# Eleven hidden-layer steps of the last chunk in seven products, with three banks, in a fused scan and feed-forward kernel

## The chip, the core and the metric

The kernel runs on one core of one Trainium2 chip. The metric is the device time in microseconds of one execution; three runs of the kernel before are given, and their median is the time to compare with. Engines are named as the profile names them: PE (TensorE, with PEld for its weight loads), DVE (VectorE), ACT (ScalarE), POOL (GpSimd) and SP (SyncE, which only issues transfers).

## What is computed

The program is a state-space scan (the "attention" block) whose output goes through a feed-forward block with a cosine gate. The feed-forward block is what the change touches:

```
# scan output y: (4, 8, 768, 32), brought to x: 3072 tokens x 256
h = x @ w_in             # 3072 x 256  times  256 x 2048
g = h * np.cos(h)
out = g @ w_out          # 3072 x 2048 times 2048 x 256
```

All numbers are float32. A float32 matrix product is two passes of a matmul on PE here: the profile shows twice as many MATMUL rows as the program has products.

## The kernel before

The 3072 tokens are cut into NC = 6 chunks (128 time steps of four sequences, 512 tokens each). A chunk's scan output lies transposed in `yT`, as two units `u` of 256 tokens with two 128-row halves `k` of the model dimension. For each chunk there are NF = 16 steps; a step `n` belongs to chunk `c = n // 16` and treats one unit `u` and one pair of 128-wide columns of `w_in`, numbered `j` (0 to 7). So the last chunk has steps 80 to 95, the last half-unit steps 88 to 95.

A step is a chain over all engines:

- `first(n)` (L650): `hp`, a PSUM bank of 128 partitions by 512, is filled by four products of 128 x 128 with 128 x 256 (two column blocks `e`, two rows `k`).
- `wind_k` (L664, ACT) and `wind_w` (L669, DVE) bring h to turns; `gate` (L679, ACT) takes the sine; `gated` (L683, DVE) makes `gT` = h times the cosine, and is the last to read the `hp` bank.
- `differ` (L707, POOL) makes four differences `gd` of the quarters of `gT` in three operations.
- `second(n)`, from chunk 1 on `seven(n)` (L741), multiplies by `w_out`. The 2 x 2 blocks of this product are done in seven block products for eight (the Winograd form of Strassen's scheme): seven products of 128 x 128 with 128 x 128, on sums and differences of blocks, accumulated in seven PSUM places over the eight steps of a half-unit. At the end of a half-unit ACT copies the places to `ps`, and `rest` (L779) makes four DVE sums of them and stores the result. The `w_out` sums (`wd`) are made once, by POOL.

The order on each engine is the order in which the Python code issues instructions; nothing is rescheduled, and waits between engines are put in by the framework from what tiles are written and read. In the main loop (L999 to L1094) step `n` issues `first(n)`, `wind(n)`, `gate(n)`, `gated(n)`, work of the scan for later chunks, and then `second(n - LAG)` with LAG = 2. So PE's row is: hp of step n, the seven products of step n - 2, hp of step n + 1, and so on.

[...] two pairs under the tag "scan" (used by the scan, and by `pair`), two banks "h" for `hp`, two banks "o" for the second layer's places. A bank taken under a tag is the one used two takings ago, so `hp` of step n waits for `gated` of step n - 2. The last half-unit takes its places `lo` and `hi` from two pairs and `mid` from a bank "o".

At the end, `shared` (L795) sums `mid` after step 94's products, and `last_step` (L807) adds the last step's product straight to the result: PE, one DVE add, two transfers, for each of two halves.

Of the kernel before, what the change touches and what calls it, by code (L numbers as in the profile page):

```python
# [25 lines left out]
def kernel(  # L26
# [17 lines left out]
    P = 128  # L44
# [630 lines left out]
    def wind(n):  # L675
        wind_k(n)
        wind_w(n)

    def gate(n):  # L679
        cos = turns[n]  # L680
        ACT.activation(cos, cos, AF.Sin, bias=quarter, scale=TWO_PI)  # L681
# [25 lines left out]
    def differ(n):  # L707
# [5 lines left out]
        G.tensor_tensor(out=d[:, 2], in0=g[:, 0], in1=d[:, 0], op=ALU.subtract)  # L713
        G.tensor_tensor(out=d[:, 3], in0=g[:, 2], in1=d[:, 2], op=ALU.subtract)  # L714

    unit_rows = out.rearrange("(s q k i) m -> q k i s m", s=2, q=2, i=W)

    def second(n):
# [20 lines left out]
    def seven(n):  # L739

        c = n // NF  # L741
        u, j = turn_of(n)
        final = n >= NC * NF - NJ
        if j == 0:


            if final:
                lo, hi = (pair("o")[:, 0].rearrange("p (q m) -> p q m", m=P) for _ in range(2))
                mid = bank([P, 4, P], "o", "o")
                o[c, u] = (mid, lo, hi, {1: mid[:, 0], 6: mid[:, 1], 7: mid[:, 2], 5: mid[:, 3],  # L750
                                         2: lo[:, 0], 3: lo[:, 1], 4: hi[:, 0]})
# [12 lines left out]
        a_ = {1: g[:, 0], 2: g[:, 2], 3: d[:, 3], 4: g[:, 3], 5: d[:, 0], 6: d[:, 2], 7: d[:, 1]}  # L764
        starts = (1, 2, 4) if final else (1, 7)
        for q in (1, 2, 6, 7, 5, 4, 3):
            PE.matmul(at[q], lhsT=a_[q], rhs=w[q], start=(j == 0 and q in starts),  # L767
                      stop=(j == NJ - 1), skip_group_check=True)
# [7 lines left out]
        ACT.copy(out=ps[:, 0:3], in_=o[c, u][0][:, 0:3])  # L776
        ACT.copy(out=ps[:, 3:7], in_=o[c, u][1])

        def rest():  # L779
            for dst, a_, b_ in ((sum_[:, 0:2], ps[:, 1:3], ps[:, 0:1]),  # L780
                                (sum_[:, 5:7], ps[:, 3:5], sum_[:, 0:1]),
                                (sum_[:, 3:5], ps[:, 5:3:-1], sum_[:, 5:6]),
                                (sum_[:, 2:3], ps[:, 6:7], sum_[:, 6:7])):
                V.tensor_tensor(out=dst, in0=a_, in1=b_.to_broadcast([P, dst.shape[1], P]),  # L784
                                op=ALU.add)
            for s in range(2):
# [155 lines left out]

    AHEAD = 4

    def first_steps():
# [53 lines left out]
    for n in range(AHEAD, NC * NF + LAG):  # L999
        c, f = divmod(n, NF)  # L1000
        if n < NC * NF:

            if c > 0 and f in (loads_of := (6, 7, 8, 9) if c == 1 else (0, 1, 2, 3)):
                load(c + 2, loads_of.index(f))
            if n in (NF - 4, NF - 3):
                load_arow(n - NF + 8)
            if n == NF - 2:
                for k in (4, 5):
                    for s in range(2):
                        load_x(k, s)  # L1010
            if n in (NF - 1, NF):
                load_along(2, (2 * (n == NF), 2 * (n == NF) + 1))
            for e, i in chunks_at(n, "along"):
                load_along(e + 1, (2 * i, 2 * i + 1))
            first(n)
            closing = f == NF - 1 and 1 <= c < NC - 1
            take_y = finish2(c + 1) if closing else None
            wind(n)
            if closing:
                take_y(0)  # L1020
            for e, s in chunks_at(n - 1, "turn"):
                turn2(e, s)
            for k in units_at(n, 2):
                turn_unit(k)
            if n + 1 in piece:
                rests_of.append(grade(*piece[n + 1], later=True))
            gate(n)
            while len(rests_of) > (n == AHEAD):
                rest = rests_of.pop(0)
                if rest:  # L1030
                    rest()
            joins = n in piece and piece[n] in held
            if joins:
                join(*piece[n])

            behind = [lambda at=at: decays2(*at) for at in decays_at(n)]
            behind += [lambda k=2 * c - 1 + i: add_state(k) for c, i in chunks_at(n, "state")]
            behind += [lambda c=c, b=2 * s + p: reaches(c, b) for c, s in chunks_at(n, "reach")
                       for p in range(2)]
            behind += [lambda at=at: turn_blocks(*at) for at in chunks_at(n, "turn")]  # L1040
            behind += [lambda k=k, p=p: decays0(k, p) for k, at in unit_at.items()
                       for p in range(2) if at[0][p] == n]
            behind = [lambda k=2 * c + i, q=q: weights(k, q) for c, i in chunks_at(n, "weigh")
                      for q in range(2)] + behind
            behind = [lambda k=k: weights(k, 1) for k in units_at(n - 1, 3)] + behind
            if not joins and behind:
                behind.pop(0)()
            gated(n)
            if closing:
                take_y(1)  # L1050
            if n == NF + 7:
                weigh0(5)
            if add_s and (n == NF - 5 or units_at(n - 1, 4)):
                exchange = add_s()
                add_s = None
            if n == NF + 9:
                exchange()
            for do in behind:
                do()
            if f not in ((10, 11, 12) if c == 1 else (10, 11)):  # L1060
                for do in unsummed:
                    do()
                unsummed.clear()
            for k, ((_, last_), *_) in unit_at.items():
                if last_ == n:
                    weigh0(k)
        for i, js in differ_at.get(n, ()):
            differ_w(i, js)
        if n == AHEAD + 1:
            second(AHEAD - LAG)  # L1070
        if n >= LAG and n != AHEAD:
# [53 lines left out]
```

## Time and profile before

| what | value |
|---|---|
| runs of the kernel before, us | 368.54, 367.84, 368.74 (median 368.54) |
| profiled execution, us | 367.37 |
| its span, from the first to the last instruction, us | 365.2 |
| granted TensorE clock | 0.999 |
| hp products (L659), busy us, count | 182.7, 768 |
| DVE `w` (L672), mean ns | 688 |
| DVE `gT` (L686), mean ns | 683 |
| ACT `k` (L666) and sine (L681), mean ns | 596 and 723 |
| POOL `gd` (L711, L713, L714), mean ns | 757, 483, 557 |

The times are of one execution with the profiler on. Lines of a timeline give the start and the time in us, the engine, the line of the kernel, the operation, what is written from what, the shape and how often; in brackets stands the idle time of the engine before it and what ended it. Lines that stand together on an engine are merged ("x8"), and then the time is that of all of them. A matmul's end is modelled and overlaps the start of the next, so the distance of starts is what counts on PE.

### The profile page before, as it was taken

The numbers are of one execution on the slowest core, as the hardware profiler recorded it, in microseconds if no ns is written. First come the engines' busy times: TensorE is split into PE (matmuls) and PEld (weight loads), VectorE is DVE, ScalarE is ACT, GpSimd is POOL, SyncE is SP. The second block draws the span as 40 slices with busy tenths as digits, with TensorE's granted clock in tenths as the row PEclk, the third lists the DMA queues.
The fourth block names the chain that finished last, engine by engine and source line by source line (L and its number), as shares of the span: only waits on it lengthen the run. The fifth ranks groups of instructions, "written<-read, shape, count | busy, mean of one in ns | idle before, by whom it ended". The sixth has DMA issues, their size and how long they took to land.

```text
span 365.2 us, 9749 instructions
## 1 busy us (share of the span) xinstructions
PE 359.7 (98%) x3902; PEld 324.8 (89%) x3902; DVE 249.6 (68%) x420; ACT 177.8 (49%) x324; POOL 204.5 (56%) x331
## 2 busy tenths in 40 slices
PE   8999999999999999999999999999999999999995
PEld 5788888888999999999989999989999999999995
DVE  7799998488868747967735977754876363644463
ACT  4588766454454355534345444335553534443442
POOL 6567666679766544447734456744355443554441
PEclk9999999999999999999999999999999999999999
DMA  8997865692664455316034210010000010010011
GB/s 146 294 334 154 203 139 72 105 129 64 133 98 65 92 106 72 69 39 121 9 56 62 47 50 22 2 44 5 22 11 0 2 31 2 2 29 3 0 29 31
DMA packets 97324, 26.39 MB, mean 72 GB/s; under 512 B 87328, under 2 KB 93184, under 8 KB 97280
## 3 DMA queue, kind: packets, MB, share of 16 engines
q1 hardware_dynamic: 96032, 25.38, 34.6%
q8 instruction: 31, 0.51, 0.6%
q10 hardware_dynamic: 1248, 0.39, 0.5%
q14 instruction: 13, 0.11, 0.1%
HBM read 22.36 MB, written 3.34 MB: 70 GB/s over the span
## 4 chain that ended last, share of the span: by engine, by line
PE 89%; DVE 4%; POOL 3%; ACT 2%; issue 2%; ACTq 0%; POOLq 0%; DVEq 0%
PE hp L659 42%; PE o L767 33%; PE o L729 5%; PE y L629 2%; PE g L603 1%; PE y L477 1%; DVE mag L261 1%; PE y L617 1%; DVE mag L263 1%; POOL gd L711 1%; PE g L456 1%; PE a_ps L364 1%; PE warm L84 1%; DVE w L672 1%; POOL gd L713 1%
## 5 line engine op out<-in xcount | busy, mean ns | idle before, releaser
L659 PE MATMUL hp<-yT,w_in 128*128 128x256 f32 x768 | 182.7, 381 | 0.3 <-DVE gT L686 0.3
L659 PEld LDWEIGHTS hp<-yT,w_in 128*128 128x128 f32 x768 | 139.5, 190 | 18.2 <-issue 1.0
L711 POOL TENSOR_TENSOR gd<-gT 128x256 f32<-128x256 f32 x79 | 59.8, 757 | 111.9 <-DVE gT L686 102.5
L672 DVE SCALAR_TENSOR_TENSOR w<-hp,k 128x512 f32<-128x512 f32 x96 | 66.1, 688 | 71.4 <-ACT k L666 71.3
L681 ACT ACTIVATE w<-w,quarter 128x512 f32<-128x512 f32 x96 | 69.4, 723 | 71.8 <-DVE w L672 71.5
L666 ACT ACTIVATE k<-hp 128x512 int32<-128x512 f32 x96 | 57.2, 596 | 94.3 <-PE hp L659 94.1
L686 DVE TENSOR_TENSOR gT<-hp,w 128x512 f32<-128x512 f32 x96 | 65.6, 683 | 35.1 <-ACT w L681 33.2
L767 PE MATMUL o<-words,gd 128*128 128x128 f32 x474 | 65.9, 275 | 0.1
L767 PEld LDWEIGHTS o<-words,gd 128*128 128x128 f32 x474 | 59.3, 192 | 0.3 <-POOL gd L713 0.3
L767 PEld LDWEIGHTS o<-w_out,gT 128*128 128x128 f32 x316 | 47.2, 191 | 4.1
L767 PE MATMUL o<-w_out,gT 128*128 128x128 f32 x316 | 48.4, 276 | 0.0
L714 POOL TENSOR_TENSOR gd<-gT,gd 128x128 f32<-128x128 f32 x79 | 44.0, 557 | 6.2
L713 POOL TENSOR_TENSOR gd<-gT,gd 128x128 f32<-128x128 f32 x79 | 38.1, 483 | 6.2
L767 PE MATMUL o<-words,gT 128*128 128x128 f32 x158 | 30.6, 275 | 0.0
L767 PE MATMUL o<-w_out,gd 128*128 128x128 f32 x158 | 30.6, 275 | 0.0
L729 PE MATMUL o<-w_out,gT 128*128 128x256 f32 x128 | 29.9, 379 | 0.0
L375 DVE TENSOR_TENSOR_SCAN lam<-arow,unit 128x512 f32<-128x512 f32 x20 | 28.0, 1400 | 0.0
L729 PEld LDWEIGHTS o<-w_out,gT 128*128 128x128 f32 x128 | 24.2, 190 | 3.3
L767 PEld LDWEIGHTS o<-words,gT 128*128 128x128 f32 x158 | 24.0, 192 | 0.0
L767 PEld LDWEIGHTS o<-w_out,gd 128*128 128x128 f32 x158 | 24.0, 192 | 0.0
L465 DVE TENSOR_TENSOR m<-g,lam 128x512 f32<-128x512 f32 x24 | 16.2, 681 | 0.7 <-PE g L456 0.5
L784 DVE TENSOR_TENSOR sum<-ps,sum 128x256 f32<-128x256 f32 (+1 forms) x27 | 15.1, 586 | 0.6
(109 smaller groups left out, 274.7 us busy)
## 6 DMA issues: line engine op xcount, KB each, us to landing
words<-in_moe_w_in_dram SPq DMA_DIRECT2D x8, 512.0 KB
words<-in_moe_w_out_dram SPq DMA_DIRECT2D x8, 512.0 KB
xr<-in_x_dram SPq DMA_DIRECT2D x24, 128.0 KB
arow<-a_cut SPq DMA_DIRECT2D x10, 256.0 KB
arow<-a_cut SPq DMA_DIRECT2D x10, 252.0 KB
out_dram<-sum SPq DMA_DIRECT2D x18, 128.0 KB
bc<-in_B_dram SPq DMA_DIRECT2D x24, 64.0 KB
blocks<-in_B_dram SPq DMA_DIRECT2D x16, 32.0 KB
```

The costliest lines, as they stand in the source:

```text
L375: V.tensor_tensor_scan(out=lams[k][:, p, hs].rearrange(flat), data0=rows_.rearrange(flat), data1=unit0[:, hs].rearrange(flat), initial=0.0 ...
L465: V.tensor_tensor(out=m, in0=gs[k, q][:, :, 0:2 * P].rearrange("p k (s i) -> p k s i", s=2), in1=l, op=ALU.mult)
L659: PE.matmul(to_[:, e], lhsT=w_in[:, k, fs], rhs=y[:, k], start=(k == 0), stop=(k == KT - 1), skip_group_check=True)
L666: ACT.activation(k, hp[n], AF.Copy, bias=0.25, scale=INV_2PI)
L672: V.scalar_tensor_tensor(out=w, in0=hp[n], scalar=INV_2PI, in1=k, op0=ALU.mult, op1=ALU.subtract)
L681: ACT.activation(cos, cos, AF.Sin, bias=quarter, scale=TWO_PI)
L686: V.tensor_tensor(out=gT[n], in0=hp.pop(n), in1=cos, op=ALU.mult)
L711: G.tensor_tensor(out=d[:, 0:2], in0=g[:, 1:2].to_broadcast([P, 2, P]), in1=g[:, 3::-3], op=ALU.subtract)
L713: G.tensor_tensor(out=d[:, 2], in0=g[:, 0], in1=d[:, 0], op=ALU.subtract)
L714: G.tensor_tensor(out=d[:, 3], in0=g[:, 2], in1=d[:, 2], op=ALU.subtract)
L729: PE.matmul(o[c, u][:, t], lhsT=g[:, 2 * e + t], rhs=w_out[:, 2 * j + e], start=(j == e == t == 0), stop=(j == NJ - 1 and e == 1), skip_gr ...
L767: PE.matmul(at[q], lhsT=a_[q], rhs=w[q], start=(j == 0 and q in starts), stop=(j == NJ - 1), skip_group_check=True)
```

## The change

In steps 83 to 93 (`sevens`, eleven of the sixteen steps of the last chunk) the first layer too is done in seven products of 128 x 128 with 128 x 128. With it come:

- `differ_in`: the sums of `w_in` blocks (`wid`), by POOL in chunk 3, sixteen operations of 128 x 256; `differ_y`: the sums of `yT` blocks of the last chunk (`yd`), four DVE operations after steps 79 and 80.
- `first7`: seven products, then an ACT copy of one of them and four DVE sums that put the four blocks of h together in the `hp` bank. Products 6, 7, 5 and 4 go to a pair of banks `m` that all eleven steps share.
- In these steps `wind_w`, `gate` and `gated` of step n are issued in step n + 1; `wind_w(n - 1)` stands between the first and the second of step n's sums, `gated(n - 1)` after the fourth.
- A third `hp` bank, from a "scan" pair, for every third of the eleven steps (85, 88), from a bank "o" for step 91. The last half-unit takes `mid` and `hi` from one pair, `lo` from a bank "o".
- The second layer's products come in another order: 1, 2, 7, 5, 6, 4, 3 in `sevens`, and 1, 2, 4, 6, 7, 5, 3 in the last half-unit.
- The sums of the half-unit that ends with step 79 stand before and after `wind_w(82)`; those of the one that ends with step 87 go to POOL, one in each of the steps 90 to 93.

```diff
+    def differ_in(i, js):
...
+        g = [win4[:, k, js, e] for k in range(2) for e in range(2)]
+        a_ = (g[1], g[1], g[0], g[2])[i]
+        b_ = (g[3], g[0], wid[0][:, js], wid[min(i, 2)][:, js])[i]
+        G.tensor_tensor(out=wid[i][:, js], in0=a_, in1=b_, op=ALU.subtract)
...
+    def differ_y(c, i):
...
+        V.tensor_tensor(out=d[:, i], in0=a_, in1=b_,
+                        op=ALU.add if i in (1, 2) else ALU.subtract)
...
+    def first7(n, to_, at6, at):
...
+        w = {1: win4[:, 0, j, 0], 2: win4[:, 1, j, 0], 3: wid[3][:, j], 4: win4[:, 1, j, 1],
+             5: wid[0][:, j], 6: wid[2][:, j], 7: wid[1][:, j]}
...
+        dst = {6: at6, 1: to_[:, 0], 7: at[:, 0], 5: at[:, 1], 4: at[:, 2], 3: to_[:, 1],
+               2: to_[:, 0]}
...
+        parts = ms[3].rearrange("p (t q m) -> p t q m", t=2, q=4)[:, n % 2]
+        add = dict(op=ALU.add)
+        for q in (6, 1):
+            product(q)
+        ACT.copy(out=parts[:, 0], in_=to_[:, 0])
+        for q in (7, 5, 4, 3, 2):
+            product(q)
+        V.tensor_tensor(out=parts[:, 1], in0=at6, in1=parts[:, 0], **add)
+
+        def rest():
+            V.tensor_tensor(out=parts[:, 2:4], in0=at[:, 0:2],
+                            in1=parts[:, 1:2].to_broadcast([P, 2, P]), **add)
+            V.tensor_tensor(out=to_[:, 2:4], in0=at[:, 2:0:-1],
+                            in1=parts[:, 2:3].to_broadcast([P, 2, P]), **add)
+            V.tensor_tensor(out=to_[:, 1], in0=to_[:, 1], in1=parts[:, 3], **add)
+
+        return rest
...
-                lo, hi = (pair("o")[:, 0].rearrange("p (q m) -> p q m", m=P) for _ in range(2))
-                mid = bank([P, 4, P], "o", "o")
+                t = pair("o").rearrange("p b (q m) -> p b q m", m=P)
+                mid, hi = t[:, 0], t[:, 1]
+                lo = bank([P, 4, P], "o", "o")
...
-        for q in (1, 2, 6, 7, 5, 4, 3):
+        for q in ((1, 2, 4, 6, 7, 5, 3) if final else (1, 2, 7, 5, 6, 4, 3) if n in sevens else
+                  (1, 2, 6, 7, 5, 4, 3)):
...
+    sevens = range(NC * NF - 13, NC * NF - 2)
+    late, at_ = [], {}
+
+    def first_of_seven(n):
+
+        i = n - sevens[0]
+        if i == 0:
+            at_["hp"] = pair("hp")[:, 0]
+            at_["m"] = pair("m").rearrange("p b (q m) -> p b q m", m=P)
+        if n == NC * NF - NJ + LAG + 1:
+            at_["hp"] = bank([P, TB], "hp", "o")
+        rest = first7(n, at_["hp"] if i % 3 == 2 else bank([P, TB], "hp", "h"),
+                      at_["m"][:, 1, 0], at_["m"][:, 0])
+        if i:
+            wind_w(late[0])
+        rest()
...
-            first(n)
+            if n in sevens:
+                first_of_seven(n)
+            else:
+                first(n)
+                if n - 1 in sevens:
+                    wind_w(n - 1)
+            if n - 1 in sevens:
+                gate(n - 1)
+            finish_late()
...
-            wind(n)
+            wind_k(n)
+            if n == sevens[0] - 1:
+                unsummed[0](range(0, 2))
+            if n not in sevens:
+                wind_w(n)
+            if n == sevens[0] - 1:
+                unsummed.pop()(range(2, 4))
...
-            gate(n)
+            if n not in sevens:
+                gate(n)
...
-            gated(n)
+            if n + 1 in sevens or n in sevens:
+                late.append(n)
+            else:
+                gated(n)
...
+            for i in {sevens[0] - 4: (0, 2), sevens[0] - 3: (1, 3)}.get(n, ()):
+                differ_y(NC - 1, i)
+            if n in sevens and unsummed:
+                i = n - sevens[-1] + 3
+                unsummed[0](range(i, i + 1), G)
+                if i == 3:
+                    unsummed.pop()
...
+        if n // NF == NC - 3:
+            i, q = divmod(f, 4)
+            differ_in(i, slice(2 * q, 2 * q + 2))
```

More of the change, by code (lines that the diff above doesn't have):

```diff
@@ L714, in differ @@
         G.tensor_tensor(out=d[:, 3], in0=g[:, 2], in1=d[:, 2], op=ALU.subtract)
+    win4 = w_in.rearrange("p k (j e f) -> p k j e f", j=NJ, e=2)
+    wid, yd = [], {}
+    def differ_in(i, js):
+        if i == len(wid):
+            t = conv.tile([P, 2 * WC, 2], U32, tag="words", bufs=8, name="wid")
+            wid.append(t.rearrange("p a w -> p (a w)").bitcast(FP32)
+                       .rearrange("p (j f) -> p j f", j=NJ))
+        g = [win4[:, k, js, e] for k in range(2) for e in range(2)]
+        a_ = (g[1], g[1], g[0], g[2])[i]
+        b_ = (g[3], g[0], wid[0][:, js], wid[min(i, 2)][:, js])[i]
+        G.tensor_tensor(out=wid[i][:, js], in0=a_, in1=b_, op=ALU.subtract)
@@ new lines, in differ_y, with product @@
+    def differ_y(c, i):
+        if i == 0:
+            yd[c] = ms[2].rearrange("p (i u m) -> p i u m", i=4, u=2)
+        d = yd[c]
+        y11, y12, y21, y22 = (yT[c][:, :, k, h * P:(h + 1) * P] for k in range(2) for h in range(2))
+        a_ = (y12, y22, y22, y21)[i]
+        b_ = (y11, y12, d[:, 0], d[:, 2])[i]
+        V.tensor_tensor(out=d[:, i], in0=a_, in1=b_,
+                        op=ALU.add if i in (1, 2) else ALU.subtract)
+    def first7(n, to_, at6, at):
+        c, f = divmod(n, NF)
+        u, j = turn_of(n)
+        hp[n] = to_
+        to_ = to_.rearrange("p (q m) -> p q m", q=4)
+        w = {1: win4[:, 0, j, 0], 2: win4[:, 1, j, 0], 3: wid[3][:, j], 4: win4[:, 1, j, 1],
+             5: wid[0][:, j], 6: wid[2][:, j], 7: wid[1][:, j]}
+        d, y = yd[c][:, :, u], yT[c][:, u].rearrange("p k (h i) -> p k h i", h=2)
+        y_ = {1: y[:, 0, 0], 2: y[:, 1, 0], 3: y[:, 1, 1], 4: d[:, 3], 5: d[:, 0], 6: d[:, 2],
+              7: d[:, 1]}
+        dst = {6: at6, 1: to_[:, 0], 7: at[:, 0], 5: at[:, 1], 4: at[:, 2], 3: to_[:, 1],
+               2: to_[:, 0]}
+        def product(q):
+            PE.matmul(dst[q], lhsT=w[q], rhs=y_[q], start=(q in (6, 1, 7)), stop=True,
+                      skip_group_check=True)
+        parts = ms[3].rearrange("p (t q m) -> p t q m", t=2, q=4)[:, n % 2]
[13 more added lines that the diff above has]
+        return rest
@@ L777, in seven, with rest @@
         ACT.copy(out=ps[:, 3:7], in_=o[c, u][1])
[L779 to L786, printed above, removed]
+        def rest(of=range(4), eng=V):
+            for dst, a_, b_ in [((sum_[:, 0:2], ps[:, 1:3], ps[:, 0:1]),
+                                 (sum_[:, 5:7], ps[:, 3:5], sum_[:, 0:1]),
+                                 (sum_[:, 3:5], ps[:, 5:3:-1], sum_[:, 5:6]),
+                                 (sum_[:, 2:3], ps[:, 6:7], sum_[:, 6:7]))[i] for i in of]:
+                eng.tensor_tensor(out=dst, in0=a_, in1=b_.to_broadcast([P, dst.shape[1], P]),
+                                  op=ALU.add)
+            for s in range(2 if 3 in of else 0):
                 nc.sync.dma_start(out=unit_rows[s, 2 * c + u], in_=sum_[s * W:(s + 1) * W, 1:5].rearrange(
@@ L943, with finish_late @@
     AHEAD = 4
+    sevens = range(NC * NF - 13, NC * NF - 2)
+    late, at_ = [], {}
+    def first_of_seven(n):
+        i = n - sevens[0]
+        if i == 0:
+            at_["hp"] = pair("hp")[:, 0]
[7 more added lines that the diff above has]
+        rest()
+    def finish_late():
+        while late:
+            n = late.pop()
+            gated(n)
     def first_steps():
@@ L1047 @@
                 behind.pop(0)()
-            gated(n)
+            if n + 1 in sevens or n in sevens:
+                late.append(n)
+            else:
+                gated(n)
             if closing:
@@ L1059 @@
                 do()
-            if f not in ((10, 11, 12) if c == 1 else (10, 11)):
+            for i in {sevens[0] - 4: (0, 2), sevens[0] - 3: (1, 3)}.get(n, ()):
[5 more added lines that the diff above has]
+                    unsummed.pop()
+            if n not in sevens and f not in ((10, 11, 12) if c == 1 else (10, 11)):
                 for do in unsummed:
```

## The prediction

> **What bounds the kernel now.** I read the busy shares first, then the chain that ended last, then the timeline of TensorE and of the others over the last chunk, where the change acts.
>
> ```profile
> PE 359.7 (98%) x3902; PEld 324.8 (89%) x3902; DVE 249.6 (68%) x420; ACT 177.8 (49%) x324; POOL 204.5 (56%) x331
> PE 89%; DVE 4%; POOL 3%; ACT 2%; issue 2%; ACTq 0%; POOLq 0%; DVEq 0%
> ...
> 315.07 1.89 PE L659 MATMUL hp<-yT,w_in 128*128 128x256 f32 x8
> 316.80 0.61 PE L767 MATMUL o<-w_out,gT 128*128 128x128 f32 x4
> ...
> 318.36 1.89 PE L659 MATMUL hp<-yT,w_in 128*128 128x256 f32 x8
> ...
> 326.93 0.60 ACT L666 ACTIVATE k<-hp 128x512 int32<-128x512 f32 x1 [1.21 <-PE hp L659]
> 327.56 0.69 DVE L672 SCALAR_TENSOR_TENSOR w<-hp,k 128x512 f32<-128x512 f32 x1 [1.05 <-ACT k L666]
> 328.28 0.72 ACT L681 ACTIVATE w<-w,quarter 128x512 f32<-128x512 f32 x1 [0.76 <-DVE w L672]
> 329.11 0.69 DVE L686 TENSOR_TENSOR gT<-hp,w 128x512 f32<-128x512 f32 x1 [0.86 <-ACT w L681]
> 329.94 0.72 POOL L711 TENSOR_TENSOR gd<-gT 128x256 f32<-128x256 f32 x1 [1.50 <-DVE gT L686]
> ```
>
> TensorE never rests: a step lasts 3.29 us (315.07 to 318.36), 1.73 for hp (16 half-width passes' worth in 8) and 1.56 for the fourteen 128-column passes of the seven products, 0.111 a pass. The second thing to see is the slack: gT follows its hp by 4.2 us, but the products that read it start a step later still, so VectorE and ScalarE wait for TensorE, never the reverse. The third is what small DVE and ACT work costs, and what a late wait costs TensorE:
>
> ```profile
> 32.86 0.68 DVE L686 TENSOR_TENSOR gT<-hp,w 128x512 f32<-128x512 f32 x1
> 33.66 1.59 PEld L659 LDWEIGHTS hp<-yT,w_in 128*128 128x128 f32 x8 [0.71 <-POOL mag L249]
> 33.69 1.97 PE L659 MATMUL hp<-yT,w_in 128*128 128x256 f32 x8 [0.33 <-DVE gT L686]
> ...
> 272.27 0.69 DVE L672 SCALAR_TENSOR_TENSOR w<-hp,k 128x512 f32<-128x512 f32 x1 [1.81 <-ACT k L666]
> 272.88 0.68 DVE L465 TENSOR_TENSOR m<-g,lam 128x512 f32<-128x512 f32 x1
> ...
> 338.15 0.72 ACT L681 ACTIVATE w<-w,quarter 128x512 f32<-128x512 f32 x1 [0.76 <-DVE w L672]
> 338.78 0.46 ACT L776 COPY ps<-o 128x384 f32<-128x384 f32 x1
> 339.14 0.59 ACT L777 COPY ps<-o 128x512 f32<-128x512 f32 x1
> ...
> 360.10 0.42 DVE L801 TENSOR_TENSOR ps<-ps 128x256 f32<-128x256 f32 x1
> 360.56 0.29 DVE L803 TENSOR_TENSOR ps<-ps 128x128 f32<-128x128 f32 x1
> 360.77 0.42 DVE L814 TENSOR_TENSOR ob<-o,ps 128x256 f32<-128x256 f32 x1
> ```
>
> A 512-column DVE operation lets the next independent one start after 0.61, a 128-column one after 0.21; a dependent one follows a 256-column add after 0.46. L814, with one operand in PSUM, takes 0.42 like L801 without. ACT's copies follow each other at 0.36 and 0.50 (their time less 0.09). When hp waited for gT, the weight load came 0.12 after gT's end (at the last step 0.05), and its matmul ran 0.1 longer, the load being bare. I take 0.08 plus 0.11.
>
> **What the Trainium skill says.** "TensorE: Matmul & The Clock Gate", "Step-by-step: what each phase is for": weight loads are pulled ahead of running matmuls, matmuls stay in program order, so one waiting product holds all behind it. The trace agrees: loads start 0.11 before their matmuls, and after the wait at 33.66 load and matmul start together. "GPSIMD Engine Reference", Specifications: GpSimd contends with DVE instructions that have two SBUF inputs. Agrees: the L784 sums took 0.41 before and about 0.70 during POOL work, while w, with one PSUM input, stayed at 0.69 beside L711. "PSUM — Partial Sum Buffer", Terms: two engines must not touch a bank at once. No run here shows a collision, but the built program's waits respect whole banks, and that decides below.
>
> **The change, part by part.** Count from T, the first pass of a seven-product hp step; products come as 6, 1, 7, 5, 4, 3, 2, two passes each.
>
> Removed: 14 passes for 16 halves, 1.73 - 1.56 = 0.17 a step, eleven steps: 1.9 us, all on the path.
>
> Added per step: one ACT copy (128 columns: by the rows of 384, 0.460, and 256, 0.379, between 0.20 and 0.30; I take 0.26) and four DVE adds of 128, 256, 256, 128 columns, each with a PSUM input. DVE has room: 0.21+0.61+0.46+0.46+0.21+0.61 = 2.56 of 3.11. Order is the trouble. On DVE a step runs: first sum, w of the step before, second, third, fourth sum, gT of the step before. In the built program the first sum waits not for product 6, which it reads, but for product 4, the last to write that pair of banks; and the next step's product 6, first in its row, waits for the third sum. So:
> - product 4's second pass issues at 9 x 0.111 = 1.00; a result was usable 0.31 (the copy of mid, at 359.15, after a pass issued at 358.84) to 0.38 (k after hp, less its longer pass) after issue: first sum at 1.34;
> - w at 1.55, second sum at 2.16, third at 2.62, its end 3.04;
> - load at 3.12, next matmul at 3.23.
>
> A step is thus 3.23, not 3.11 (bounds 3.17 and 3.30 from the spreads above). The fourth sum starts at 3.08, ends 3.37; gT starts 3.29, ends 3.98; k runs 3.40 to 4.00. In that rhythm the other waits are met: the copy at 0.68 to 0.94 comes just before product 3's load at 1.00; gT's POOL work (0.73, 0.46, 0.46, begun 0.15 after gT) ends 2.7 into the next step, product 3 of the second layer loads at 2.9.
>
> Four hand-overs don't fit the rhythm.
> - Step 83 to 84: hp 84 takes the bank of hp 82, whose gT now stands behind step 83's sums. T is 315.07; the third sum waits for product 2 (316.86), runs at 317.20, fourth 317.66, gT 317.87 to 318.56. Product 1 of step 84 goes at 318.75 for 318.40: this step is 3.46. The output sums now around w of 82 push that w from 314.40 by at most 0.35; product 3 of step 83 would absorb that in the same wait.
> - Step 90: two ps copies of the finished half-unit stand in ACT's row between k of 89 (0.15 on) and the copy of 90. They begin at 0.66 and 1.02, the copy at 1.52, ending 1.78; product 3 goes at 1.93 for 1.11: 3.93.
> - Step 93 to 94: hp 94 takes the bank of hp 92, two steps back, not three. gT of 92 ends 3.98 into step 93; plus 0.19: 4.15, where 3.11 was due.
> - Step 94 on is as before, 3.29; in steps 92 and 93 the second layer's new order asks for POOL's third difference 0.22 earlier, 0.14 late, mostly inside the 0.12 already lost: 3.24.
>
> Sum from 83 to 95: 3.46 + 6 x 3.23 + 3.93 + 2 x 3.24 + 4.15 + 3.29 = 40.69, before 12 x 3.29 = 39.48: plus 1.2 us.
>
> Elsewhere: sixteen POOL subtractions of 128x256 (0.73 to 0.83, as L705) in chunk 3. POOL is busy 1.65 of each 3.29 there, so nothing waits; around 205 us DVE is full and gT ended 207.37 with hp at 207.62, so a stretched sum could cost 0.1 once: 0 to 0.2, I take 0. Four DVE adds for yd after gT of 79 and 80, about 0.45 to 0.7 each, in gaps of 2.2 and 1.05: 0. The last output sums move to POOL behind each difference, with a step in hand: 0; their two output transfers issue about 13 us before the end. At the end the copy of mid comes two passes later (0.22), and the first ob at 360.99 instead of 360.77; the second waits for TensorE at 361.50 anyway: 0 (0.05 if the transfers' issues touch).
>
> The profiled execution took 367.37, its span 365.2 plus 2.2 around it; the forecast makes it 368.6. The median, 368.54, is 1.2 above that execution, so on the median: 369.8. No change can be told within 0.3%, 1.1 us, that is 367.4 to 369.65.
>
> **Rivals.**
> - B, the sums keep up: waits resolve in the lower bounds or PE's queue hides them, and steps run at 3.11. Then six and two steps save 0.12 each, step 90 loses a little more (k comes later against it), step 94 the same: plus 0.5, 369.0. For it: the margin is 0.12. Against: every term has a row.
> - C, ends on the other side: the first sum goes when product 6 and the copy are done (1.02), because the wait on product 4 is met without the delay I give it. Everything on DVE comes 0.32 earlier: 3.11 for step 83 and the six, step 90 about 3.72, two of 3.11, step 93 3.81, then 3.29: 38.8, minus 0.7, 367.9. It decides as soon as the third sum ends before 2.9. Against it stands the wait as built.
> - D, POOL stretches the sums: if the second sum, beside POOL's differences, takes 0.70 as L784 did, a step is 3.51; eight of them, and step 93, add 2.5: 372.3. Against: one input is in PSUM, and w beside L711 was not stretched.
> - That the change doesn't do what it says is excluded by its order: eleven steps have 14 passes.
>
> **How the numbers follow.** Forecast 0.62, own range 369.0 to 370.9 (steps of 3.17 to 3.30, the hand-overs give or take 0.1 each); a third of it lies under 369.65. B 0.15, C 0.09, D 0.14. Slower: 0.41 + 0.14 = 0.55. Within: 0.21 + 0.15 + 0.05 = 0.41. Faster: 0.04 of C. The range takes most of B and part of C and D: 368.3 to 371.8.
>
> **What would show it.** The seven hp products busy 1.56 a step; the step's period in steps 84 to 89 (3.11 refutes my loop, 3.2 confirms it); "TensorE waited for DVE" at the first product of each step, longest, about 1 us, at step 94; a wait for ACT of about 0.8 at step 90; sums of 256 columns at 0.42, not 0.70. A period of 3.11 with short hand-overs makes the prediction wrong to the fast side, a stretched second sum to the slow side.

## The result, and the profile after

The changed kernel takes 370.49 us (median of 8 runs, 369.79 to 371.56), the kernel before, run beside it, 368.34 (8 runs, 367.73 to 369.41). The ratio is 1.0056, with a 95% interval of 1.0039 to 1.0073: slower, by about 2 us. It lies in the predicted range, on the predicted side, 0.7 us above the predicted 369.8; the range, 368.3 to 371.8, was wide enough to hold the time of the kernel before too. The profiled execution has a span of 368.0 us for 365.2.

The page of the changed kernel, busy shares and then the chain that ended last:

```profile
PE 360.2 (98%) x3968; PEld 326.6 (89%) x3968; DVE 264.2 (72%) x464; ACT 179.6 (49%) x335; POOL 219.1 (60%) x351
...
PE 85%; DVE 6%; POOL 3%; ACT 3%; issue 2%; DVEq 0%; ACTq 0%; POOLq 0%
```

TensorE is still busy 98% of the time, and this share hides what was lost: a 128-column pass is shown with 0.275 us where the next follows after 0.111, so short gaps between passes are covered. What it can't cover is the idle rest of the span, 7.8 us (368.0 less 360.2) where it was 5.5. The chain shows more. TensorE's share falls from 89 to 85%, and VectorE's rises from 4 to 6%: there are now places where the end of the kernel hangs on VectorE.

Where these places are is seen in the timeline of the changed kernel. From it I put lines of five windows together: chunk 3, step 86, step 90, the turn from step 93 to 94, and the end. (A merged line shows the shape of its first instruction; the third of the three sums of chunk 3 is 128x128.) The columns are start, duration, engine, line, operation, and in brackets the idle time before with what ended it. L758 is a product of the seven-product hp, L765 the copy, L768, L771, L773 and L775 the first to fourth sum.

```profile
203.78 1.90 DVE L849 TENSOR_TENSOR sum<-ps,sum 128x256 f32<-128x256 f32 x3
204.62 0.91 POOL L730 TENSOR_TENSOR wid<-w_in 128x256 f32<-128x256 f32 x1
205.60 0.68 DVE L672 SCALAR_TENSOR_TENSOR w<-hp,k 128x512 f32<-128x512 f32 x1
207.16 0.67 DVE L686 TENSOR_TENSOR gT<-hp,w 128x512 f32<-128x512 f32 x1
207.98 1.97 PE L659 MATMUL hp<-yT,w_in 128*128 128x256 f32 x8 [0.41 <-DVE gT L686]
...
325.61 0.47 PE L758 MATMUL m<-m,wid 128*128 128x128 f32 x2
325.92 0.39 PE L758 MATMUL hp<-yT,w_in 128*128 128x128 f32 x2
325.97 0.60 ACT L666 ACTIVATE k<-hp 128x512 int32<-128x512 f32 x1 [0.54 <-DVE hp L775]
326.46 0.26 ACT L765 COPY m<-hp 128x128 f32<-128x128 f32 x1
326.59 0.39 PE L758 MATMUL m<-m,w_in 128*128 128x128 f32 x2
327.08 0.29 DVE L768 TENSOR_TENSOR m<-m 128x128 f32<-128x128 f32 x1 [0.62 <-PE m L758]
327.29 0.68 DVE L672 SCALAR_TENSOR_TENSOR w<-hp,k 128x512 f32<-128x512 f32 x1
327.89 0.41 DVE L771 TENSOR_TENSOR m<-m 128x256 f32<-128x256 f32 x1
328.41 0.43 DVE L773 TENSOR_TENSOR hp<-m 128x256 f32<-128x256 f32 x1
328.90 0.49 PE L758 MATMUL m<-m,wid 128*128 128x128 f32 x2
...
339.17 0.60 ACT L666 ACTIVATE k<-hp 128x512 int32<-128x512 f32 x1 [0.54 <-DVE hp L775]
339.67 0.47 ACT L841 COPY ps<-o 128x384 f32<-128x384 f32 x1
340.03 0.60 ACT L842 COPY ps<-o 128x512 f32<-128x512 f32 x1
340.50 0.30 ACT L765 COPY m<-hp 128x128 f32<-128x128 f32 x1
340.85 0.49 PE L758 MATMUL hp<-yT,wid 128*128 128x128 f32 x2 [0.67 <-ACT m L765]
...
352.95 0.68 DVE L686 TENSOR_TENSOR gT<-hp,w 128x512 f32<-128x512 f32 x1
353.78 1.97 PE L659 MATMUL hp<-yT,w_in 128*128 128x256 f32 x8 [0.83 <-DVE gT L686]
...
363.64 0.88 DVE L879 TENSOR_TENSOR ob<-o,ps 128x256 f32<-128x256 f32 x2
```

What to see there:

- **The rhythm.** Step 86 runs from 325.61 to 328.90, 3.29 us: exactly what a step took before the change, though its hp now has 14 passes of 128 columns for what were 8 of 256. VectorE stands idle 0.62 until product 4 releases the first sum (327.08, product 4 having started at 326.59), then goes from one sum to the next, with w between them, to the third, which ends at 328.84; the next step's first product goes 0.06 later.
- **Step 90.** ScalarE works off k, two ps copies and then the copy of hp. Product 3 waits 0.67 for it.
- **Step 94.** Its hp, again of the old form, was kept waiting 0.83 until gT of step 92 had read its bank.
- **Chunk 3**, a hundred microseconds before the seven-product steps: hp waited 0.41 for a gT that came late, with VectorE's three output sums just before it at 1.90 us together (1.36 before the change), and GpSimd's new subtraction (L730) beside the last of them.
- **The end.** The two ob adds now touch, where they stood 0.73 apart (360.77 and 361.50) before.

Step lengths of all kernels, named by the headings of the next section, from first pass to first pass on TensorE; 204 and 208 us are two neighbouring hp steps of chunk 3, "last step" is `last_step`, counted from its first pass to the end of the span (spans read to the hundredth: 365.22 before, 367.99 after), and the last column is the median of the spans of all executions of that kernel:

| kernel | 204 to 208 | 83 + 84 | 85 to 89, each | 90 | 91 + 92 | 93 | 94 | 83 to 95 | last step to end | median span |
|---|---|---|---|---|---|---|---|---|---|---|
| before | 3.29 | 6.58 | 3.29 | 3.29 | 6.58 | 3.29 | 3.29 | 39.48 | 5.76 | 365.6 |
| forecast | 3.29 | 6.69 | 3.23 | 3.93 | 6.48 | 4.15 | 3.29 | 40.69 | 5.76 to 5.81 | |
| after | 3.87 | 6.79 | 3.30 | 4.16 | 6.53 | 4.29 | 3.36 | 41.64 | 5.93 | 368.7 |
| w first | 3.87 | 6.72 | 3.13 | 3.76 | 6.27 | 3.74 | 3.36 | 39.51 | 5.95 | 366.6 |
| copy first | 3.86 | 6.79 | 3.30 | 3.33 | 6.60 | 4.29 | 3.37 | 40.89 | 6.23 | 368.0 |
| bank of 94 | 3.87 | 6.80 | 3.30 | 4.16 | 6.52 | 3.30 | 3.30 | 40.58 | 5.96 | 367.6 |
| POOL spread | 3.29 | 6.79 | 3.30 | 4.16 | 6.53 | 4.29 | 3.36 | 41.64 | 5.94 | 367.9 |
| after again | 3.87 | 6.79 | 3.30 | 4.16 | 6.53 | 4.29 | 3.36 | 41.64 | 5.94 | 368.7 |
| ps later | 3.86 | 6.80 | 3.30 | 3.32 | 6.60 | 4.29 | 3.37 | 40.88 | 5.94 | 367.8 |
| gT of 82 | 3.86 | 6.78 | 3.30 | 4.16 | 6.53 | 4.29 | 3.36 | 41.63 | 5.94 | 368.7 |
| all five | 3.29 | 6.34 | 3.27, then 3.13 | 3.13 | 6.26 | 3.14 | 3.29 | 37.96 | 5.95 | 364.3 |
| all but gT of 82 | 3.29 | 6.72 | 3.13 | 3.13 | 6.26 | 3.14 | 3.29 | 38.20 | 5.95 | 364.6 |
| all five and end | 3.29 | 6.33 | 3.28, then 3.14 | 3.14 | 6.28 | 3.14 | 3.29 | 38.00 | 5.76 | 364.1 |

Counted from 204.33 (before) and 204.11 (after), the start of the same hp step in chunk 3, to the end of the span, the profiled execution after takes 163.88 and that before 160.89: 2.99 us more. The terms are 0.58 and 0.07 in chunk 3, 2.16 from step 83 to 95 and 0.17 at the end (2.98, the rest is rounding). Nothing else moved. The stretch before was 0.22 shorter in the profiled execution after, and that is chance, as will be seen.

The medians of whole runs differ by only 2.1. A time holds more than its span, and this remainder is not the same for the two: in every execution whose span is on record it is 1.7 to 1.9 us for the changed kernel and for the kernels made from it, and 2.1 to 2.8 for the kernel before. No run here shows why. So part of what the span lost is not seen in the time. Between the two profiled executions that part is 0.4 us; in the later runs of both, side by side, it is 0.7, the medians of the spans (368.7 and 365.6) differing by 3.1, close to the sum of the terms, and those of the times by 2.4. The spans are given to 0.1 us; the last two kernels ran on another chip, where that of the kernel before was 365.5. One slow execution each of w first (373.80) and of the last kernel (371.46) is left out of their medians; the latter is the one profiled, but its loss lies before 126 us and its steps from 83 on are as long as in the kernels beside it.

### The profile page after: what moved, and what is told of

Read it like the earlier page. It is cut to its first block, busy times and chain, and to the rows that moved or that the text cites. A ratio compares the mean times of both kernels' runs of the same rounds, so it can differ in the third digit from the quotient of the medians.

```text
span 368.0 us, 9977 instructions
## 1 busy us (share of the span) xinstructions
PE 360.2 (98%) x3968; PEld 326.6 (89%) x3968; DVE 264.2 (72%) x464; ACT 179.6 (49%) x335; POOL 219.1 (60%) x351
## 4 chain that ended last, share of the span: by engine, by line
PE 85%; DVE 6%; POOL 3%; ACT 3%; issue 2%; DVEq 0%; ACTq 0%; POOLq 0%
PE hp L659 35%; PE o L832 31%; PE o L792 5%; PE m L758 3%; PE hp L758 2%; PE y L629 2%; PE g L603 1%; DVE w L672 1%; DVE mag L261 1%; PE y L477 1%; PE y L617 1%; DVE gT L686 1%; ACT k L666 1%; POOL gd L713 1%; POOL gd L711 1%
## 5 line engine op out<-in xcount | busy, mean ns | idle before, releaser
L659 PE MATMUL hp<-yT,w_in 128*128 128x256 f32 x680 | 162.1, 382 | 1.6 <-DVE gT L686 1.6
L659 PEld LDWEIGHTS hp<-yT,w_in 128*128 128x128 f32 x680 | 123.6, 190 | 18.1 <-PE o L832 1.6
L832 PE MATMUL o<-words,gd 128*128 128x128 f32 x474 | 66.0, 275 | 0.1
L832 PEld LDWEIGHTS o<-words,gd 128*128 128x128 f32 x474 | 59.2, 192 | 0.3 <-POOL gd L713 0.3
L832 PEld LDWEIGHTS o<-w_out,gT 128*128 128x128 f32 x316 | 46.4, 191 | 3.6
L832 PE MATMUL o<-w_out,gT 128*128 128x128 f32 x316 | 48.4, 276 | 0.0
L713 POOL TENSOR_TENSOR gd<-gT,gd 128x128 f32<-128x128 f32 x79 | 40.5, 513 | 6.2
L714 POOL TENSOR_TENSOR gd<-gT,gd 128x128 f32<-128x128 f32 x79 | 40.5, 512 | 6.2
L832 PE MATMUL o<-w_out,gd 128*128 128x128 f32 x158 | 30.6, 275 | 0.0
L832 PE MATMUL o<-words,gT 128*128 128x128 f32 x158 | 30.5, 275 | 0.0
L792 PEld LDWEIGHTS o<-w_out,gT 128*128 128x128 f32 x128 | 24.2, 190 | 3.3
L832 PEld LDWEIGHTS o<-w_out,gd 128*128 128x128 f32 x158 | 24.0, 192 | 0.0
L832 PEld LDWEIGHTS o<-words,gT 128*128 128x128 f32 x158 | 24.0, 192 | 0.0
L271 POOL TENSOR_TENSOR w_out<-mag,last 128x512 uint32<-128x512 uint32 x8 | 10.2, 1273 | 9.1 <-DVE mag L263 9.1
```

The lines of the kernel that those rows point to most:

```text
L659: PE.matmul(to_[:, e], lhsT=w_in[:, k, fs], rhs=y[:, k], start=(k == 0), stop=(k == KT - 1), skip_group_check=True)
L792: PE.matmul(o[c, u][:, t], lhsT=g[:, 2 * e + t], rhs=w_out[:, 2 * j + e], start=(j == e == t == 0), stop=(j == NJ - 1 and e == 1), skip_gr ...
```

## The experiments

All are the changed kernel with the edits named; times are medians, and ratios are to the kernel before on the same chip. My theory: the rhythm is a loop through VectorE (product 4, first sum, w, second and third sum, next product 6), and beside it there are three hand-overs and the crowding in chunk 3. The rivals stand with each.

### w of the step before ahead of the first sum

```diff
+        if before:
+            before()
         V.tensor_tensor(out=parts[:, 1], in0=at6, in1=parts[:, 0], **add)
...
-                      at_["m"][:, 1, 0], at_["m"][:, 0])
-        if i:
-            wind_w(late[0])
+                      at_["m"][:, 1, 0], at_["m"][:, 0],
+                      (lambda: wind_w(late[0])) if i else None)
         rest()
```

> w of the step before goes ahead of the first sum on VectorE; nothing else moves. Theory (the loop through VectorE sets the step: product 4, first sum, w, second and third sum, next product 6): k is ready about 1.0 after a step's start, so w runs at 1.0, the first sum at 1.65 for 1.47, but the third sum ends at about 2.9 for 3.24. Steps 85 to 89 fall from 3.30 to between 3.11 and 3.20 (what is left is the wait for the copy at product 3, 0.07), the wait of step 94 shortens by 0.3 to 0.4, the whole kernel by 1.0 to 1.8 us against the changed one. Rival (TensorE loses the time inside its own row, through bare loads and the copy): steps stay within 0.04 of 3.30, the kernel within 0.4 of the changed one.

Measured: 368.34 us (21 runs), ratio to before 1.0015 (0.9999 to 1.0031). Steps 85 to 89 fell to 3.13, step 90 to 3.76, step 93 to 3.74. From 83 to 95 the kernel became 2.13 us shorter, a little more than expected; so did the median of the spans, by 2.1. The timeline of this kernel, step 86 (lines L770, L773, L775 are now the first to third sum) and the two late waits:

```profile
326.00 0.60 ACT L666 ACTIVATE k<-hp 128x512 int32<-128x512 f32 x1 [1.03 <-PE o L834]
326.03 0.39 PE L758 MATMUL m<-m,wid 128*128 128x128 f32 x2
326.63 0.69 DVE L672 SCALAR_TENSOR_TENSOR w<-hp,k 128x512 f32<-128x512 f32 x1
327.42 0.29 DVE L770 TENSOR_TENSOR m<-m 128x128 f32<-128x128 f32 x1
327.75 0.42 DVE L773 TENSOR_TENSOR m<-m 128x256 f32<-128x256 f32 x1
328.27 0.43 DVE L775 TENSOR_TENSOR hp<-m 128x256 f32<-128x256 f32 x1
329.16 0.39 PE L758 MATMUL m<-m,wid 128*128 128x128 f32 x2
...
340.21 0.49 PE L758 MATMUL hp<-yT,wid 128*128 128x128 f32 x2 [0.37 <-ACT m L765]
...
352.33 1.97 PE L659 MATMUL hp<-yT,w_in 128*128 128x256 f32 x8 [0.45 <-DVE gT L686]
```

k of the step before ends at 326.60 and w follows at once, in the time in which VectorE had stood waiting for product 4. The third sum ends at 328.70, 0.46 before the next step needs it, and the step takes 3.13, or 28 passes of 0.112: TensorE sets the pace again. VectorE works in the order in which it is given its work: in the changed kernel w, ready at 326.57, stood until 327.29 behind a first sum that was itself waiting. That one place in the row costs 2.13 us, as much as the change lost between 83 and 95 (2.16). The rival, a loss inside TensorE's own row, falls: the weight loads that started late and the wait of product 3 went away with the loop, so they were its consequence.

### k behind the step's copy

```diff
+    sevens_ = range(NC * NF - 13, NC * NF - 3)
...
         ACT.copy(out=parts[:, 0], in_=to_[:, 0])
+        if n - 1 in sevens_:
+            wind_k(n - 1)
...
-            wind_k(n)
+            if n not in sevens_:
+                wind_k(n)
```

> k of the step before goes behind the step's copy on ScalarE, not ahead of it. Then product 3 has no reason to wait for the copy (0.07 a step). Theory (VectorE's loop sets the step): the wait at product 3 goes, the one at the next product 6 grows by as much, steps 85 to 89 stay at 3.28 to 3.32. Rival (ScalarE's row is part of what sets the step): steps fall to 3.22 to 3.24. The kernel differs from the changed one by less than 0.3 us by the first, is 0.5 to 0.7 shorter by the second.

Measured: 369.80 us (5 runs), ratio 1.0054 (1.0041 to 1.0067). Product 2 follows product 3, the one that waited for the copy, after 0.23 and no longer after 0.29, and the step stays at 3.30. ScalarE's row does not set it. What I had not expected: step 90 falls from 4.16 to 3.33, because k no longer stands ahead of the two ps copies and the copy comes before product 3 needs it. The trace is 0.75 us shorter from 83 to 95, though its end, where the first ob add comes 0.28 later than in the others, gives 0.3 back. The median of the spans is 0.7 shorter; the timed ratio does not show it, within its interval.

### hp of step 94 in the third bank

```diff
-        hp[n] = bank([P, TB], "hp", tag) if tag else pair("hp")[:, 0]
+        hp[n] = at_["hp"] if n == NC * NF - 2 else bank([P, TB], "hp", tag) if tag else pair("hp")[:, 0]
```

> hp of step 94 goes into the third bank, three steps old, and not into that of hp 92, two steps old. Theory (step 93 to 94 waits for that bank alone): the step of 4.29 falls to 3.2 to 3.35 and the kernel by 0.9 to 1.1 us against the changed one. Rival (gT of 92 is late for the second layer too, or the third sum of 93 holds the row): only part goes, the step stays above 3.6, the kernel falls by less than 0.7.

Measured: 369.34 us (5 runs), ratio 1.0046 (1.0034 to 1.0058). The step falls from 4.29 to 3.30, the stretch from 83 to 95 by 1.06, the median of the spans by 1.1. The hand-over was that bank alone. The ratio, beside 1.0056 and 1.0065 for the changed kernel, fell by 0.4 to 0.7 us only, less than expected; within the intervals of the ratios it can be 1.1.

### GpSimd's subtractions spread

```diff
-        if n // NF == NC - 3:
-            i, q = divmod(f, 4)
+        m = n - NF * (NC - 3)
+        m = m - 5 if 5 <= m < NF else m - 10 if NF + 5 <= m < NF + 10 else NF
+        if 0 <= m < NF:
+            i, q = divmod(m, 4)
             differ_in(i, slice(2 * q, 2 * q + 2))
```

> GpSimd's sixteen subtractions of w_in are spread over steps 5 to 15 of chunk 3 and 5 to 9 of chunk 4, so that the first five steps of chunk 3, where VectorE is full, have none. Theory (GpSimd's subtractions stretched VectorE's scan and sums with two SBUF inputs there, so that gT came late for hp): the wait of hp for gT near 208 us goes, step 83 starts about 0.43 earlier, as in the kernel before, and the kernel is 0.3 to 0.6 us shorter than the changed one. Rival (something else put the 0.43 there, as another chance state of the DMAs): step 83 starts within 0.1 of 315.50.

Measured: 369.67 us (7 runs), ratio 1.0062 (1.0039 to 1.0085). Step 83 starts at 315.53, which is what the rival said; but that was a bad yardstick. This execution reached its first large hp at 34.22 us and the one after the change at 33.81, and the step in dispute shows what the edit did. Its timeline:

```profile
204.29 1.36 DVE L849 TENSOR_TENSOR sum<-ps,sum 128x256 f32<-128x256 f32 x3
205.57 0.68 DVE L672 SCALAR_TENSOR_TENSOR w<-hp,k 128x512 f32<-128x512 f32 x1
207.13 0.68 DVE L686 TENSOR_TENSOR gT<-hp,w 128x512 f32<-128x512 f32 x1
208.08 1.89 PE L659 MATMUL hp<-yT,w_in 128*128 128x256 f32 x8
```

The three sums take 1.36 again, the bracket at hp is gone, and the step from 204.79 to 208.08 is 3.29. The three do not share the loss. By shape (count, then busy us and mean ns of one), first after the change, then in the kernel before:

```profile
L849 DVE TENSOR_TENSOR sum<-ps,sum 128x256 f32<-128x256 f32 x2 | 1.1, 562 | 0.1
L849 DVE TENSOR_TENSOR sum<-ps,sum 128x128 f32<-128x128 f32 x1 | 0.8, 811 | 0.0
...
L784 DVE TENSOR_TENSOR sum<-ps,sum 128x256 f32<-128x256 f32 x2 | 1.1, 560 | 0.1
L784 DVE TENSOR_TENSOR sum<-ps,sum 128x128 f32<-128x128 f32 x1 | 0.3, 279 | 0.0
```

The two larger sums stood beside GpSimd's differences already before, and took 0.56 in both kernels, where such a sum that began while GpSimd stood idle took 0.42 (at 313.75 in the profile after). So the 0.58 was the subtractions' doing: in the one step in which VectorE had no time left they stretched one sum with two operands in SBUF from 0.28 to 0.81, and the second of two scans before it from 0.26 to 0.76, of which 0.17 came through to the sums. This is what the Trainium skill says in "GPSIMD Engine Reference", section Specifications (GpSimd's path to SBUF contends with VectorE instructions of two SBUF inputs), and here its price shows. That the whole kernel became shorter by that much is not shown by the times, whose interval holds both; the median of the spans is 0.8 shorter, which fits it.

### The changed kernel again, on the chip of the next three

> The changed kernel itself, on the chip of the next three. Its ratio to before should fall into 1.004 to 1.007. Of the step lengths those from 83 to 95 and the 0.58 near 208 us should repeat to 0.03 (if they are the program's), the places before 38 us and near 121 us, where the kernels so far differ by up to 0.5, should not (if they are chance).

Measured: 370.49 us (21 runs), ratio 1.0065 (1.0048 to 1.0081). All lengths of the table repeat to 0.03. The start does not: first large hp 34.25 (33.81 in the profile after), and the hp step near 121 us 5.04 (5.10; 5.28 in the kernel before, 5.01 to 5.28 in the others). So the hp step that starts at 204.11 in the profile after starts here at 204.54, for no reason in the kernel; and in the profile of gT of 82 an hp step near 102 us took 5.72, for 4.52 to 4.58 in those above. Nearly all of this lies before 126 us, and positions later in the trace carry it along. Lengths of steps are to be compared, not positions.

### ps copies behind the copy of step 90

```diff
-        ACT.copy(out=ps[:, 0:3], in_=o[c, u][0][:, 0:3])
-        ACT.copy(out=ps[:, 3:7], in_=o[c, u][1])
+        def save():
+            ACT.copy(out=ps[:, 0:3], in_=o[c, u][0][:, 0:3])
+            ACT.copy(out=ps[:, 3:7], in_=o[c, u][1])
+
+        if n == NC * NF - NJ - 1:
+            unsaved.append(save)
+        else:
+            save()
...
         ACT.copy(out=parts[:, 0], in_=to_[:, 0])
+        if unsaved:
+            unsaved.pop()()
```

> The two copies of the finished half-unit to ps go behind the copy of step 90. Theory (they hold up step 90 in ScalarE's row, and nothing needs them earlier: product 2 of the second layer, the first to write one of the copied banks, comes 1.8 into the step, the copy is through at 1.5): step 90 falls from 4.16 to 3.25 to 3.35, the kernel by 0.8 to 0.9 us against the changed one. Rival (the wait moves to that product 2, or to w of 89 times a quarter behind the copies): step 90 and 91 together fall by less than 0.5.

Measured: 369.59 us (22 runs), ratio 1.0035 (1.0019 to 1.0052), beside 1.0065 for the changed kernel on the same chip. Step 90 is 3.32, 0.84 less. Steps 91 and 92, with 6.60 between them for 6.53, took 0.07 of it back, and nothing more of the wait moved on.

### gT of step 82 ahead of the sums of step 83

```diff
-            if n + 1 in sevens or n in sevens:
+            if n in sevens:
                 late.append(n)
```

> gT of step 82 goes ahead of the sums of step 83 on VectorE. Theory (step 84 waits for the bank of hp 82 because its gT stands behind those sums): product 1 of step 84 follows product 6 after 0.22 and not 0.53, steps 83 and 84 together take 6.45 to 6.5 for 6.79, the kernel is 0.3 us shorter. Rival (w of 82 times a quarter is late anyway and pushes the sums of 83 by the same): 83 and 84 stay above 6.7.

Measured: 370.53 us (22 runs), ratio 1.0055 (1.0041 to 1.0069): no gain, and steps 83 and 84 take 6.78. The theory missed, and the rival's number came true without its mechanism. Product 1 of step 84 came after 0.23, as the theory said, and w of 82 held nothing up, against the rival (the sums of 83 came 0.2 later, behind gT itself, and step 84 began no later for that). The timeline (L771 and L773 are the second and third sum of step 84) shows where the gain went:

```profile
320.36 0.39 PE L758 MATMUL hp<-yT,w_in 128*128 128x128 f32 x2
...
322.33 0.42 DVE L771 TENSOR_TENSOR m<-m 128x256 f32<-128x256 f32 x1
...
323.22 0.43 DVE L773 TENSOR_TENSOR hp<-m 128x256 f32<-128x256 f32 x1 [0.47 <-PE o L832]
323.68 0.30 DVE L775 TENSOR_TENSOR hp<-hp,m 128x128 f32<-128x128 f32 x1
323.70 0.49 PE L758 MATMUL m<-m,wid 128*128 128x128 f32 x2 [0.28 <-DVE hp L773]
```

The third sum begins 0.89 behind the second, for 0.52 in the other steps and in this step of the changed kernel. The profile puts 0.47 of idle time there down to a product of the second layer (L832), which writes neither its operands nor its destination. The next step waits for that sum.

### The five together, and without the last

> Five edits in one: w ahead of the first sum, step 94 in the third bank, GpSimd's subtractions spread, ps copies behind the copy of step 90, gT of 82 ahead of the sums. Theory (the waits found are all there is): from the first pass of step 83 to that of 95 38.0 to 38.3 us (before 39.48, the change 41.64), the 0.58 near 208 us gone, ratio to before 0.995 to 0.998. Rival (a wait removed is taken up by the next one, as VectorE has no time left): above 39.0, ratio 0.999 or more.

> The five edits without that of gT of 82, which gave nothing alone: there product 1 of step 84 came 0.31 sooner, but the third sum of step 84 began 0.89 behind the second for 0.52, so that step 85 started no earlier. Theory (the edit pays once w goes ahead of the first sum, since VectorE then has time to spare in step 84): without it steps 83 and 84 take 6.72 as with w ahead alone, for 6.34; step 85 takes 3.13, for 3.27; the way from 83 to 95 grows by 0.24 to 38.2. Rival (the edit is worth nothing here either): it stays at 37.9 to 38.0.

Measured: all five 366.07 us (13 runs), ratio to before 0.9939 (0.9917 to 0.9960); without gT of 82 366.36 us (10 runs), 0.9958 (0.9943 to 0.9972). From 83 to 95 it is 37.96 with it and 38.20 without, as the theories said (within 0.04). The ratio of all five is a little under the expected 0.995, which made nothing of the time outside the span. The edits add up: 39.51 with w ahead alone, less 0.60 in step 93, 0.63 in step 90, 0.24 for gT of 82 and 0.07 in step 94, is 37.97. And gT of 82, worth nothing alone, is worth 0.24 where VectorE has time to spare: it shortens 83 and 84 by 0.38 and gives 0.14 back in step 85, since the late third sum of step 84 is there too (0.88 behind the second). The page of the five together:

```profile
PE 358.3 (98%) x3968; PEld 325.6 (89%) x3968; DVE 264.1 (73%) x464; ACT 180.2 (50%) x335; POOL 218.6 (60%) x351
...
PE 88%; DVE 4%; SPq 3%; ACT 2%; issue 1%; POOL 1%; DMA 0%; ACTq 0%; DVEq 0%
```

Nearly the same instructions in another order: VectorE's share of the chain is back at 4%, and the kernel beats the one before by 1.5 to 2.3 us (by the ratios of these two and the next kernel). Of this the spans hold 0.9 to 1.4 (their medians, each beside the kernel before on its chip); the rest is the shorter time outside the span, which the changed kernel has too and which no order of instructions here accounts for. In the traces 1.52 of the 1.76 us that eleven shorter steps are worth (0.16 each) is found between 83 and 95, and 0.19 of it goes back at the end.

### The last half-unit's products in another order

```diff
-        for q in ((1, 2, 4, 6, 7, 5, 3) if final else (1, 2, 7, 5, 6, 4, 3) if n in sevens else
+        for q in ((1, 4, 6, 7, 5, 2, 3) if final else (1, 2, 7, 5, 6, 4, 3) if n in sevens else
```

> The five edits, and in the last half-unit the second layer's products in the order 1, 4, 6, 7, 5, 2, 3: the pair of banks that holds 1, 4, 5, 6, 7 is then full two passes earlier, so that its copy to ps can start 0.22 earlier, as in the kernel before. Theory (the two passes cost the end 0.2, since the four transfers of the last two output blocks then issue close together): from the first pass of the last step to the end of the span 5.7 to 5.8 for 5.93, the kernel 0.2 shorter. Rival (the second block waits for TensorE anyway): 5.9 or more, no difference.

Measured: 365.88 us (6 runs), ratio 0.9946 (0.9925 to 0.9967). The copy of mid starts 0.25 before the last step and not 0.03, the two ob adds stand 0.67 apart again, and from the last step's first pass to the end it is 5.76 for 5.95, what it was in the kernel before. The theory holds in the trace at 0.19; the times of the two kernels can't be told apart.

## Why the prediction was right, and where it was not

Point by point, in the order of the prediction.

- **The gain, 1.9 us.** Right: where nothing holds TensorE up (w first), a step is 3.13 for 3.29: 0.16 a step, or 1.76 for eleven.
- **The rhythm, 3.23 a step; measured 3.30.** The mechanism is the predicted one, term by term, and w first took the loop apart at its weakest link, the place of w. Two terms were sized too small. The first sum came 1.47 after the step's start for 1.34: product 4 issued 0.09 later, since after the wait the second pass of product 6 came 0.20 behind the first and not 0.11, and its result was usable after 0.38, the upper of my two bounds, not after the 0.34 in the middle. And the third sum follows the second after 0.52 where I had taken 0.46 from adds whose operands all lie in SBUF (L801); these two have one operand in PSUM, and the third writes there too; which of the two makes the 0.06 was not tested. Against that the next product goes 0.06 behind the third sum, not 0.19: the 0.11 for a bare load (a weight load that no running product hides) is there, as 0.09, but I had counted it in the hand-over, and it sits inside the next step.
- **Step 83 to 84, 6.69 with the next; measured 6.79.** The wait for gT of 82 is there (product 1 0.53 behind product 6), but taking it away alone gained nothing, since the third sum of step 84 then came late; with w first it was worth 0.24.
- **Step 90, 3.93; measured 4.16.** Right mechanism. The row of ScalarE began 0.2 later, at 0.87, since k follows a fourth sum that ends at 0.28 into the step.
- **Step 93 to 94, 4.15; measured 4.29.** Right, with the step's own lateness on top; bank of 94 settles it.
- **Steps 91, 92 and 94.** 6.53 for 6.48, and 3.36 for 3.29: after the wait a bare load costs 0.07 more.
- **Chunk 3, "0 to 0.2, I take 0"; measured 0.58.** This step failed. I saw that VectorE was full there and that a stretched sum could cost, but priced one stretched sum at 0.1. One was hit indeed, but by 0.53: all but 0.01 of the 0.54 by which the three grew is in the third. The scans before them gave 0.17 more; gT had 0.25 us to spare (207.37 to 207.62), and the late gT's hand-over with its bare load gave 0.12 on top: 0.58.
- **The end, 0 to 0.05; measured 0.17.** I had named the transfers that touch, and found too little. The first ob add comes 0.28 later after the last step's first pass (1.58 for 1.30) and the second when it did before (2.03), but its two transfers, which issued at 2.48, now stand behind the first two and issue at 2.62 and 2.67.
- **The rivals.** B and C are out by the 3.30, C also by the 0.62 for which the first sum stood until product 4. D is out: the second sum took 0.41 beside GpSimd's differences, which fits its operand in PSUM.

The forecast's plus 1.2 was 3.0 in the profile and 2.1 in the medians. Of the 1.8 missing in the profile, 0.65 is chunk 3, 0.95 the terms between 83 and 95, and 0.17 the end. That the time still came within 0.7 of the forecast is in part luck: the forecast kept the 2.2 us that the kernel before spends around its span, and the changed kernel spends 1.8. What the runs confirm is the mechanism, the loop and the hand-overs, more than the number.

Two things stay open: why the changed kernel spends less time outside its span, and why the third sum of step 84 begins 0.36 late in the kernels that move gT of 82. What it needs, the second sum and product 2, was done by then, and no run here tells the cause.

## What to carry to other kernels

An engine that is busy 72% of the time can set the pace: if its row holds an instruction that waits, and behind it one that is ready, the step grows by the waiting, so when work is added to such a row, put the ready work ahead of the waiting work before anything else. Work given to GpSimd is to be laid where VectorE has time to spare, or has an operand in PSUM. And compare lengths of steps between traces, never positions: two executions of one kernel here were 0.43 us apart before the change began. A time and a span are not to be mixed either: here they moved by different amounts.

## What was not expected of the hardware

- A VectorE sum or scan with both operands in SBUF stood still until GpSimd was through. In the profile after, 36 of them (L849 and L574) began while a GpSimd instruction was running, and each ended 0.28 (256 columns) or 0.14 to 0.15 (sums of 128, scans of 64) after that instruction did. So a sum of 128 columns took 0.54 or 0.81, and 0.28 when GpSimd was idle, and a scan up to 0.77 for some 0.26: the price is what is left of GpSimd's instruction, not a share of VectorE's. A sum of 128x256 with one operand in PSUM kept its 0.41 beside GpSimd's differences.
- After a wait of TensorE, the product behind the waiting one was 0.31 after it where 0.22 is the rhythm: one wait costs 0.09 beyond its own length.
- A 256-column VectorE add with one operand in PSUM was followed by one that depends on it, and writes to PSUM, after 0.52; with all in SBUF it was 0.46.
